# Batch 1's column norms summed on VectorE and GpSimd instead of by TensorE

## The chip, the cores and the metric

One core of one Trainium2 chip. The metric is the device time of one execution in microseconds (us), as the median of several. The profile is one execution; its span is some 2 us shorter than the device time.

## The reference

Two stages: an attention over channels (the softmax of a 256 x 256 matrix per batch, built from normalised q and k) and a feed-forward layer with a maximum over three products.

```python
B, N, C = (4, 6144, 256)
qn = q / (np.linalg.norm(q, axis=1, keepdims=True) + 1e-06)   # norm over the 6144 tokens
kn = k / (np.linalg.norm(k, axis=1, keepdims=True) + 1e-06)
s = kn.transpose(0, 2, 1) @ qn / tau
a = softmax(s)                                                 # ... cut
x = (v @ a).reshape(B * N, C)
h = np.maximum(np.maximum(x @ w1, x @ w2), x @ w3)             # d_ff = 768
out = h @ w_out
```

The kernel folds `a` into the weights (`aw = a @ w`), so that each chunk of 512 tokens needs only `v @ aw`, the maximum, and `@ w_out`. There are 12 chunks per batch. While a batch runs, the next one's q and k are loaded, squared for the norms, and multiplied into the Gram matrix `k^T q`.

## The kernel before

The norms need, per channel, a sum of squares over 128 partitions x 48 token groups. ScalarE squares three groups at a time, GpSimd adds the pieces into an accumulator and folds it to 256 columns, and then something has to add over the 128 partitions. For batch 1 that was TensorE, with a matrix of ones; for batches 2 and 3 ("early", squares run one chunk sooner) it is GpSimd.

```python
def norms(b):                       # batch 1: TensorE adds over the partitions
    n_ps = htile("n_ps")
    accq, acck = accs.pop((b, 0)), accs.pop((b, 1))
    PE.matmul(n_ps[:, :C], lhsT=ones_f, rhs=acck[:, 0:C], ...)
    for j in range(CC):
        PE.matmul(n_ps[:, C + j:C + j + 1], lhsT=accq[:, j * P:(j + 1) * P], rhs=ones_f[:, 0:1], ...)
    # ... cut: Ln and Exp on ScalarE give rkb and rq

def sum_all(b):                     # batches 2 and 3: GpSimd adds over the partitions
    for which in range(2):
        acc = accs[b, which]
        tot = sm.tile([P, C], FP32, name=f"tot{which}")
        POOL.partition_all_reduce(tot, acc[:, 0:C], P, bass_isa.ReduceOp.add)
        accs[b, which] = tot

def norms_all(b):                   # batches 2 and 3: VectorE picks q's diagonal, then Ln, Exp
    for j in range(CC):
        DVE.tensor_tensor_reduce(out=scr, in0=totq[:, j * P:(j + 1) * P], in1=ident, ...,
                                 accum_out=n2q[:, j:j + 1])
    # ... cut: Ln, Exp of totk -> rkb; Ln, Exp of n2q -> rq
```

A chunk is six hidden blocks. Each takes six matmuls into three PSUM buffers; ScalarE copies the first, VectorE takes the maximum with the second and then with the third. Between the blocks, in "gaps", other work is slipped in: the output products of the chunk before, and at the end of a batch the next batch's norms, the scaling of the Gram (`scaled`), the exponential and the row sums. The Gram itself runs as one burst of 48 matmuls ahead of the last chunk. Hidden blocks share six PSUM buffers, the Gram and the output products share two. (PSUM is the memory that TensorE writes its results to; copying a result out of it is called an eviction here. A "weight product" is a part of `a @ w`, a "fold" adds the three 256-column pieces of an accumulator into one, and a "diagonal pick" takes q's sums from a full tile into one column.)

## Time and profile before

| | before |
|---|---|
| device time, median of the executions timed beside the changed kernel | 574.09 us (574.03 to 574.11) |
| span of the profiled execution | 572.1 us (its device time: 573.92 us) |
| TensorE busy | 553.9 us, 97% |
| VectorE, ScalarE, GpSimd busy | 411.1, 309.1, 235.1 us |
| Gram burst of batch 1 starts | 151.75 us |

A timeline line reads: start in us, length in us, engine, line of the program, operation, output <- inputs, shapes, number of instructions merged, and in brackets the idle time before it and what ended it. PE is TensorE, PEld its weight load, DVE VectorE, ACT ScalarE, POOL GpSimd. As TensorE is nearly always busy, only its own order and its waits matter; the prediction shows the lines.

### The profile page before, as it was taken

The numbers are of one execution on the slowest core, as the hardware profiler recorded it, in microseconds if no ns is written. First come the engines' busy times: TensorE is split into PE (matmuls) and PEld (weight loads), VectorE is DVE, ScalarE is ACT, GpSimd is POOL, SyncE is SP. The second block draws the span as 40 slices with busy tenths as digits, with TensorE's granted clock in tenths as the row PEclk, the third lists the DMA queues.
The fourth block names the chain that finished last, engine by engine and source line by source line (L and its number), as shares of the span: only waits on it lengthen the run. The fifth ranks groups of instructions, "written<-read, shape, count | busy, mean of one in ns | idle before, by whom it ended". The sixth has DMA issues, their size and how long they took to land.

```text
span 572.1 us, 9442 instructions
## 1 busy us (share of the span) xinstructions
PE 553.9 (97%) x3349; PEld 330.7 (58%) x3350; DVE 411.1 (72%) x647; ACT 309.1 (54%) x539; POOL 235.1 (41%) x240
## 2 busy tenths in 40 slices
PE   3799999999999999999999999999999999999997
PEld 2665555555755555555575555555575555555566
DVE  0048777877577777777768777777868778778775
ACT  1044567677454576776545467767645444444443
POOL 2443357776730078776560048777750000000000
PEclk9999999999999999999999999999999999999999
DMA  9998998884598168984179339885437323132112
GB/s 143 106 146 129 136 237 126 159 135 116 99 107 160 56 107 158 134 148 110 57 128 151 99 81 140 148 141 98 124 86 154 75 75 109 56 103 64 56 55 76
DMA packets 76960, 65.64 MB, mean 115 GB/s; under 512 B 52464, under 2 KB 62576, under 8 KB 76784
## 3 DMA queue, kind: packets, MB, share of 16 engines
q0 software_dynamic: 19072, 26.48, 38.7%
q1 hardware_dynamic: 57696, 38.41, 23.7%
q8 instruction: 26, 0.43, 0.3%
q14 instruction: 22, 0.18, 0.1%
q10 hardware_dynamic: 144, 0.13, 0.1%
HBM read 78.64 MB, written 25.17 MB: 181 GB/s over the span
## 4 chain that ended last, share of the span: by engine, by line
PE 93%; DMA 5%; POOL 0%; issue 0%; DVE 0%; POOLq 0%
PE h_ps L389 65%; PE o_ps L409 22%; DMA q_sb<-in_q_dram 5%; PE gram L260 3%; PE ew_ps L311 3%; POOL k_sb L99 0%; PE o_ps L434 0%; PE ew_ps L335 0%; PE warm_ps L469 0%; PE vt_ps L372 0%; PE gram L177 0%; PE n_ps L215 0%; DVE ht_sb L395 0%; DVE o_sb L461 0%; PE n_ps L217 0%
## 5 line engine op out<-in xcount | busy, mean ns | idle before, releaser
L389 PE MATMUL h_ps<-vt_sb,aw_sb 128*128 128x512 bf16 (+1 forms) x1764 | 406.7, 375 | 0.1
L389 PEld LDWEIGHTS <-aw_sb 128*128 128x128 bf16 x1764 | 171.8, 98 | 161.3 <-DVE aw_sb L317 2.0
L394 DVE TENSOR_TENSOR s_mx<-h_ps,s_mx 128x512 bf16<-128x512 f32 (+1 forms) x294 | 198.7, 676 | 87.1 <-ACT s_mx L393 86.8
L393 ACT ACTIVATE s_mx<-h_ps 128x512 bf16<-128x512 f32 (+1 forms) x294 | 172.4, 587 | 124.9 <-PE h_ps L389 124.0
L395 DVE TENSOR_TENSOR ht_sb<-h_ps,s_mx 128x512 bf16<-128x512 f32 (+1 forms) x294 | 200.2, 681 | 31.4 <-PE o_ps L409 0.5
L203 POOL TENSOR_TENSOR acc<-acc,sq 128x768 f32<-128x768 f32 x90 | 147.6, 1651 | 70.5 <-ACT sq L197 61.6
L409 PE MATMUL o_ps<-wo_sb,ht_sb 128*128 128x256 bf16 x1128 | 153.9, 273 | 0.0
L409 PEld LDWEIGHTS <-ht_sb 128*128 128x128 bf16 x1128 | 110.4, 98 | 52.0
L412 ACT ACTIVATE o_sb<-o_ps 128x512 f32<-128x512 f32 x94 | 56.1, 597 | 85.3 <-PE o_ps L409 85.3
L110 POOL DMA_DIRECT2D v_sb<-in_v_dram x48 | 27.5, 578 | 37.7 <-DMA vt_sb<-v_sb 35.5
L197 ACT ACTIVATE sq<-q_sb 128x768 bf16<-128x768 fp8e4 x48 | 40.5, 845 | 0.0
L197 ACT ACTIVATE sq<-k_sb 128x768 bf16<-128x768 fp8e4 x48 | 40.1, 835 | 0.0
L200 POOL CAST acc<-sq 128x768 f32<-128x768 bf16 x6 | 4.9, 823 | 68.7 <-ACT sq L197 68.7
L102 POOL DMA_DIRECT2D q_sb<-in_q_dram x33 | 18.4, 564 | 5.1 <-DMA v_sb<-in_v_dram 4.1
L165 PE MATMUL kk<-k_sb 128*128 128x256 fp8e4 x48 | 7.5, 338 | 11.9 <-DVE k_sb L151 6.3
L99 POOL DMA_DIRECT2D k_sb<-in_k_dram x29 | 16.1, 555 | 3.1 <-DMA v_sb<-in_v_dram 1.2
L260 PE MATMUL gram<-k_sb,q_sb 128*128 128x512 fp8e4 x144 | 16.8, 277 | 0.0
L260 PEld LDWEIGHTS <-q_sb 128*128 128x256 fp8e4 x144 | 15.9, 136 | 0.6
L314 ACT ACTIVATE aw_sb<-ew_ps,rinv 128x384 bf16<-128x384 f32 (+1 forms) x24 | 13.2, 555 | 5.5 <-PE ew_ps L311 4.7
L311 PE MATMUL ew_ps<-w_sb,et 128*128 128x384 bf16 (+1 forms) x96 | 15.6, 313 | 0.0
L177 PE MATMUL gram<-k_sb,q_sb 128*128 128x512 fp8e4 x48 | 11.4, 332 | 2.6 <-DMA q_sb<-in_q_dram 2.4
L165 PEld LDWEIGHTS <-k_sb 128*128 128x256 fp8e4 x48 | 6.4, 182 | 12.9 <-DMA k_sb<-in_k_dram 6.6
(67 smaller groups left out, 112.9 us busy)
## 6 DMA issues: line engine op xcount, KB each, us to landing
out_dram<-o_sb SPq DMA_DIRECT2D x41, 512.0 KB, 2.9
v_sb<-in_v_dram POOLq DMA_DIRECT2D x48, 256.0 KB, 4.2
k_sb<-in_k_dram POOLq DMA_DIRECT2D x24, 192.0 KB, 6.0
q_sb<-in_q_dram POOLq DMA_DIRECT2D x24, 192.0 KB, 7.6
out_dram<-o_sb SPq DMA_DIRECT2D x13, 256.0 KB, 2.0
k_sb<-in_k_dram POOLq DMA_DIRECT2D x5, 256.0 KB, 10.8
w_sb<-in_moe_w_dram POOLq DMA_DIRECT2D x9, 128.0 KB, 5.7
kf<-in_k_dram SPq DMA_DIRECT2D x1, 1024.0 KB, 4.8
```

Of the source, the lines that this page charges most:

```text
L102: POOL.dma_start(out=qk[b][0][:, g0:g0 + w, :], in_=q_r[b][:, g0:g0 + w, :])
L110: POOL.dma_start(out=t, in_=v_r[gi // NCH, gi % NCH])
L197: ACT.activation(out=sq, in_=src, func=AF.Square)
L203: POOL.tensor_tensor(out=acc, in0=acc, in1=sq, op=ALU.add)
L260: PE.matmul(g[:, j * C:(j + 1) * C], lhsT=qt[:, tsl, j * P:(j + 1) * P], rhs=kt[:, tsl, :], start=(tp == 0 and j == 0), stop=(tp == NG // ...
L311: PE.matmul(ew[:, :w], lhsT=et[:, j, ic * P:(ic + 1) * P], rhs=w_sb[m][:, j, fsl], start=(j == 0), stop=(j == CC - 1))
L389: PE.matmul(t.rearrange("p (t n) -> p t n", n=P), lhsT=aw[m][:, ic, fsl], rhs=vt[:, tsl, ic, :], start=(ic == 0), stop=(ic == CC - 1))
L393: ACT.activation(out=s_mx, in_=hp[0], func=AF.Copy)
L394: DVE.tensor_tensor(out=s_mx, in0=hp[1], in1=s_mx, op=ALU.max)
L395: DVE.tensor_tensor(out=ht, in0=hp[2], in1=s_mx, op=ALU.max)
L409: PE.matmul(st["ps"][:, half], lhsT=ht[:, fc, t * P:(t + 1) * P], rhs=wo_sb[:, fc, :], start=(fc == 0), stop=(fc == FC - 1))
L412: ACT.activation(out=st["o"][:, t - 1:t + 1, :].rearrange("p t d -> p (t d)"), in_=st["ps"], func=AF.Copy)
```

## The change

The intent is to take the norm matmuls of batch 1 off TensorE. GpSimd alone would be too late for it (an estimate: in the kernel before its folds end at 154.53 + 3.02 = 157.55 us, about 6 us for its library and 3.6 us for two sums would follow, to near 167 us, and ScalarE took up the norms at 159.46), so VectorE adds the last two q squares and does the folds while it is idle in the Gram burst, and a dummy sum makes GpSimd take up its library a chunk ahead.

```diff
+    zero = consts.tile([P, 4], FP32, name="zero")
+    DVE.memset(zero, 0.0)
+    lib = consts.tile([P, 4], FP32, name="lib")
...
-    def norms(b):                       # the TensorE version goes; norms_all is renamed norms
-        n_ps = htile("n_ps")
...
+                    last = not early and s0 == 7 and which == 0
+                    # ... the last q squares of batch 1 are left in a list
             if more and s0 == 7:
-                gaps[5].append(lambda: fold(b + 1))
                 if early:
-                    gaps[5].append(lambda: sum_all(b + 1))
+                    gaps[5].append(lambda: (fold(b + 1, POOL), sum_all(b + 1)))
+                else:
+                    gaps[3].append(lambda: POOL.partition_all_reduce(lib, zero, P, bass_isa.ReduceOp.add))
...
-                    gaps[0].append(lambda: st.update(n=norms(b + 1)))
-                    gaps[1].append(lambda: st.update({"in": scaled(gs, st["n"][0])}))
-                    gaps[2].append(lambda: st.update(e=exp_t(st["in"], st["n"][1])))
+                    gaps[1].append(lambda: st.update(n=norms(b + 1)))
+                    gaps[2].append(lambda: st.update({"in": scaled(gs, st["n"][0])}))
+                    gaps[3].append(lambda: st.update(e=exp_t(st["in"], st["n"][1])))
...
             if more and ch == NCH - 2:
                 if early:
-                    st["n"] = norms_all(b + 1)
+                    st["n"] = norms(b + 1)
+                else:
+                    for which, sq in left:
+                        acc = accs[b + 1, which]
+                        DVE.tensor_tensor(out=acc, in0=acc, in1=sq, op=ALU.add)
+                    fold(b + 1, DVE)
+                    sum_all(b + 1)
                 gs = gram_kq(b + 1)
```

More of the change, by code (lines that the diff above doesn't have):

```diff
@@ L192, with square_piece @@
     accs = {}
-    def square_piece(b, which, g0):
+    def square_piece(b, which, g0, leave=None):
         src = qk[b][which][:, g0:g0 + SQW, :].rearrange("p g c -> p (g c)")
@@ L197, in square_piece @@
         ACT.activation(out=sq, in_=src, func=AF.Square)
-        if g0 == 0:
+        if leave is not None:
+            leave.append((which, sq))
+        elif g0 == 0:
             accs[b, which] = sm.tile([P, SQW * C], FP32, name=f"acc{which}")
@@ L203, in square_piece, with fold @@
             POOL.tensor_tensor(out=acc, in0=acc, in1=sq, op=ALU.add)
-    def fold(b):
+    def fold(b, engine):
         for which in range(2):
@@ L208, in fold @@
             for i in range(1, SQW):
-                POOL.tensor_tensor(out=acc[:, 0:C], in0=acc[:, 0:C], in1=acc[:, i * C:(i + 1) * C], op=ALU.add)
-    def norms(b):
-        n_ps = htile("n_ps")
-        accq, acck = accs.pop((b, 0)), accs.pop((b, 1))
-        PE.matmul(n_ps[:, :C], lhsT=ones_f, rhs=acck[:, 0:C], start=True, stop=False, skip_group_check=True)
-        for j in range(CC):
-            PE.matmul(n_ps[:, C + j:C + j + 1], lhsT=accq[:, j * P:(j + 1) * P], rhs=ones_f[:, 0:1],
-                      start=False, stop=(j == CC - 1), skip_group_check=True)
-        ln = sm.tile([P, C + CC], FP32, name="ln")
-        rkb = sm.tile([P, C], FP32, name="rkb")
-        rq = sm.tile([P, CC], FP32, name="rq")
-        ACT.activation(out=ln, in_=n_ps[:, :C + CC], func=AF.Ln)
-        ACT.activation(out=rkb, in_=ln[:, :C], func=AF.Exp, scale=-0.5)
-        ACT.activation(out=rq, in_=ln[:, C:], func=AF.Exp, scale=-0.5, bias=neg_ln_tau)
-        return rkb, rq
+                engine.tensor_tensor(out=acc[:, 0:C], in0=acc[:, 0:C], in1=acc[:, i * C:(i + 1) * C], op=ALU.add)
     def sum_all(b):
@@ L233, in sum_all, with norms @@
             accs[b, which] = tot
-    def norms_all(b):
+    def norms(b):
         totq, totk = accs.pop((b, 0)), accs.pop((b, 1))
@@ L487 @@
     pending = []
+    left = []
     for b in range(B):
@@ L522 @@
                 for i, (which, g) in enumerate(((1, g0), (1, g0 + SQW), (0, g0), (0, g0 + SQW))):
-                    gaps[(0, 2, 3, 5)[i]].append(lambda which=which, g=g: square_piece(b + 1, which, g))
+                    last = not early and s0 == 7 and which == 0
+                    gaps[(0, 2, 3, 5)[i]].append(
+                        lambda which=which, g=g, last=last: square_piece(b + 1, which, g, left if last else None))
             if more and s0 == 7:
-                gaps[5].append(lambda: fold(b + 1))
                 if early:
-                    gaps[5].append(lambda: sum_all(b + 1))
+                    gaps[5].append(lambda: (fold(b + 1, POOL), sum_all(b + 1)))
+                else:
+                    gaps[3].append(lambda: POOL.partition_all_reduce(lib, zero, P, bass_isa.ReduceOp.add))
             if more and ch == NCH - 1:
```

## The prediction

> **What bounds the kernel now.** I read the page first: engines, then the chain that ended last.
>
> ```profile
> PE 553.9 (97%) x3349; PEld 330.7 (58%) x3350; DVE 411.1 (72%) x647; ACT 309.1 (54%) x539; POOL 235.1 (41%) x240
> PE 93%; DMA 5%; POOL 0%; issue 0%; DVE 0%; POOLq 0%
> ```
>
> TensorE is busy for 97% of the span and is 93% of the chain, at full granted clock in every slice. So the change can only win TensorE time it removes or bubbles it closes, and can only lose by making TensorE wait. It touches one place, the end of batch 0, where batch 1's norms are made; batches 2 and 3 already use the other method (sums over partitions on GpSimd). So the timeline of TensorE there for batch 1, and then for batch 2, which shows what the same stretch costs without the norm matmuls:
>
> ```profile
> 157.19 1.47 PE L389 MATMUL h_ps<-vt_sb,aw_sb 128*128 128x512 bf16 x6
> 158.49 0.59 PE L215 MATMUL n_ps<-acc,ones_f 128*128 128x256 f32 x2
> 158.92 0.50 PE L217 MATMUL n_ps<-ones_f,acc 128*128 128x1 f32 x4
> 159.29 1.45 PE L389 MATMUL h_ps<-vt_sb,aw_sb 128*128 128x512 bf16 x6
> ...
> 168.48 2.11 PE L311 MATMUL ew_ps<-w_sb,et 128*128 128x384 bf16 x12
> ...
> 291.98 2.76 PE L389 MATMUL h_ps<-vt_sb,aw_sb 128*128 128x512 bf16 x12
> ...
> 302.48 2.11 PE L311 MATMUL ew_ps<-w_sb,et 128*128 128x384 bf16 x12
> ```
>
> From the first hidden-block matmul after the Gram to the first weight product: 168.48 - 157.19 = 11.29 us in batch 1, 302.48 - 291.98 = 10.50 us in batch 2. The difference, **0.79 us**, is the gap that the norm matmuls make (159.29 - 158.49 = 0.80). Nothing else in TensorE's order differs.
>
> Then the timeline of GpSimd and of VectorE in the model, batch 2:
>
> ```profile
> 278.93 3.01 POOL L209 TENSOR_TENSOR acc<-acc 128x256 f32<-128x256 f32 x4
> 287.99 3.61 POOL L232 PARTITION_ALL_REDUCE tot<-acc  x2 [6.05 <-issue]
> ...
> 289.84 1.22 DVE L241 CUSTOM_DVE_ANT_0 scr<-tot,ident 128x128 f32<-128x128 f32 x1 [1.59 <-POOL tot L232]
> 290.98 0.08 DVE L241 DVE_READ_ACCUMULATOR2_ANT n2q<- 128x1 f32 x1
> 291.09 0.29 DVE L241 CUSTOM_DVE_ANT_0 scr<-tot,ident 128x128 f32<-128x128 f32 x1
> ```
>
> Before the first sum over partitions GpSimd stands still 6.05 us with nothing to wait for (5.69 us in batch 3): taking up its library. Each sum takes 1.8 us. And on batch 1's side:
>
> ```profile
> 148.42 3.25 POOL L203 TENSOR_TENSOR acc<-acc,sq 128x768 f32<-128x768 f32 x2 [2.17 <-ACT sq L197]
> 152.80 1.64 POOL L203 TENSOR_TENSOR acc<-acc,sq 128x768 f32<-128x768 f32 x1 [1.14 <-ACT sq L197]
> 154.53 3.02 POOL L209 TENSOR_TENSOR acc<-acc 128x256 f32<-128x256 f32 x4
> ```
>
> **What the Trainium skill says.** "GPSIMD Engine Reference", section 2.1 Instruction dispatch: the first call to a freshly loaded kernel pays a load of about 6 us, with no visible instruction. The trace agrees (6.05 and 5.69 us of idle). Same page, section 3.1: a two-input add takes GpSimd 1.96 times as long as VectorE. The trace has no such VectorE add; I use the ratio as an estimate. "SBUF — State Buffer", section SBUF: two separate sides: a VectorE operation with two SBUF inputs and a GpSimd operation that reads SBUF hold a shared port pair against each other. The trace agrees: the first diagonal pick above took 1.22 us beside a sum over partitions, the second 0.29 us; and GpSimd's adds beside VectorE's one-SBUF-input maxima keep 1.634 to 1.684 us over all 90.
>
> **The change, step by step.** *Removed from TensorE*: six fp32 matmuls, 0.79 us. This is on the path and is the whole possible gain.
>
> *Library.* The dummy sum is queued on GpSimd behind the last k square's add, which ends at about 148.42 + 1.64 = 150.06. The load then runs to 150.06 + 6.05 = 156.1. The dummy reads 4 columns, so at most the 1.8 us of a real one; I take 1.0. GpSimd is ready at 157.1.
>
> *VectorE in the Gram burst.* It is idle from 153.45 (end of the last maximum) to 158.46, as the Gram holds TensorE from 151.75 to 157.2. It gets two 768-column adds, estimated 1645/1.96 = 0.84 us, and four folds, estimated 726/1.96 = 0.37 us. With 0.1 us between dependent ones that is about 2 x 0.94 + 4 x 0.47 = 3.8 us: q is ready at 156.3, k at 157.2, a microsecond before VectorE is needed. Free.
>
> *Sums.* q from 157.1 to 158.9, k to 160.7. VectorE's diagonal picks are in its queue behind the maxima of block 1. Without the norm matmuls these are at 159.86 and 160.65 (spacings 0.79 and 0.61 as elsewhere); the picks start at 161.26, after both sums, take 2 x 0.3 us, and give n2q at 161.9. ScalarE has Ln and Exp for k done by 161.5; Ln and Exp for q follow at 161.93 and 162.14, and block 2's copy starts at 162.25 instead of 161.07 (its place in batch 2: 295.87 less the offset of 134.80 between the Grams). So ScalarE is some 1.2 us late, with six PSUM buffers, two blocks, to absorb it: block 4 needs block 2's buffers from 164.33; they come free at 162.8, 163.6 and 164.4 against needs of 164.3, 164.8 and 165.2. Free.
>
> *Scaling.* It moves from behind block 1 to behind block 2 on VectorE: 164.27 to 165.02. From here VectorE runs without a gap: maxima of block 3 at 164.93 and 165.72, block 4 at 166.33 and 167.12, reciprocal 167.73, block 5 at 167.89 and 168.68, so its three weight evictions start at 169.29. Without any lateness they would start at 169.84 - 0.79 = 169.05. This **0.24 us** does reach TensorE, for the next batch's first block waits for exactly these evictions already (timeline of weight loads, before):
>
> ```profile
> 171.03 0.14 PEld L389 LDWEIGHTS <-aw_sb 128*128 128x128 bf16 x2 [0.29 <-DVE aw_sb L317]
> 171.56 0.10 PEld L389 LDWEIGHTS <-aw_sb 128*128 128x128 bf16 x1 [0.38 <-DVE aw_sb L317]
> ```
>
> *Later.* GpSimd must take its usual library back at the second batch's first add. It did so before batch 3's squares (idle 6.99 us) while TensorE kept its rhythm of 10.39 us per chunk, so that is hidden. Its V, K and Q loads start some 3 us later, five chunks ahead of use: hidden.
>
> Sum: -0.79 + 0.24 = -0.55 us, or 573.55 us; with something for the port lock between the dummy and VectorE's adds (below), **573.6 us**.
>
> **The rivals.** (1) *The Gram's PSUM buffer becomes a wait.* Gram and output accumulators share two buffers. Before, the third output product of that chunk takes the Gram's buffer, free once scaling ended at 163.06. If it still does, it is wanted at 163.68 and free at 165.05: TensorE stalls 1.4 us, and the kernel ends at about 574.7 (-0.79 + 1.38). Against it: the buffers seem to be handed out in the order in which they come free, and the scaling, one block later, now comes behind ScalarE's copy of the first output half, so that buffer should be taken. I give the stall one chance in five. (2) *The library comes late.* If the load drags (transposes fill the DMA from 152 to 155; the very first library use, at 4.75 us under full DMA, waited 11.0 us), the sums end later, ScalarE stands in Ln, and every microsecond beyond about 0.4 is passed through block 2 to TensorE: 2 us late is some 574.7, 5 us late 577 to 578. For it: that start; against: both 6 us loads, and that the DMA is quiet until 152. One in six. (3) *Port lock*: the dummy can wait for one VectorE add, up to 0.9 us; the sums then end at 161.5, the picks start in their tail, and a further 0.3 us of lateness goes to the weight evictions: 573.9. (4) *All hidden*, the evictions catching up: 573.3.
>
> **Range and chances.** The best possible is 574.1 - 0.79 = 573.3. The middle cases are 573.5 to 573.9, the two bad ones 574.7 and more. So 573.2 to 574.8 should hold it 8 times in 10. Two per cent is 11.5 us, more than ten times what is at stake either way; only a library load gone badly wrong could reach it. Faster 0.002, same 0.99, slower 0.008.
>
> **What would show it right or wrong.** Right: no n_ps lines; a GpSimd idle of about 6 us that starts near 150 and the two sums ending by about 161; VectorE's adds inside the Gram burst, ended by 157.5; the stretch from first hidden block to first weight product 10.5 us; the weight loads' waits on the evictions grown by about a quarter of a microsecond. Wrong: an output product waiting for VectorE's scaled Gram (rival 1); ScalarE's Ln waiting for the sums for over 1.5 us (rival 2); diagonal picks over 0.5 us (rival 3). A time under 573.2 would mean that something outside this stretch moved too.

## The result, and the profile after

The changed kernel takes 573.67 us (573.67 to 573.75, four executions) against 574.09 us (574.03 to 574.11, four). The ratio, computed as the mean time of one kernel's fast runs over that of the other's of the same rounds (so not quite the ratio of the medians), is 0.9993, with a 95% interval of 0.9976 to 1.0011. The four executions of each kernel do not overlap: 0.42 us lie between the medians.

The page of the changed kernel, its engine line:

```profile
PE 552.9 (97%) x3344; PEld 329.1 (58%) x3344; DVE 415.9 (73%) x658; ACT 309.1 (54%) x540; POOL 233.3 (41%) x237
```

TensorE lost 1.0 us of busy time, VectorE gained 4.8 us. A share of busy time says nothing here; the stretch around the Gram does. TensorE's timeline of the changed kernel there (the hidden blocks' line is now L378, the output products' L398, the weight products' L300):

```profile
157.62 2.76 PE L378 MATMUL h_ps<-vt_sb,aw_sb 128*128 128x512 bf16 x12
...
162.82 1.46 PE L378 MATMUL h_ps<-vt_sb,aw_sb 128*128 128x512 bf16 x6
164.12 0.82 PE L398 MATMUL o_ps<-wo_sb,ht_sb 128*128 128x256 bf16 x6
...
168.12 2.11 PE L300 MATMUL ew_ps<-w_sb,et 128*128 128x384 bf16 x12
170.07 1.65 PE L378 MATMUL h_ps<-vt_sb,aw_sb 128*128 128x512 bf16 x6
171.55 2.11 PE L300 MATMUL ew_ps<-w_sb,et 128*128 128x384 bf16 x12
173.50 1.46 PE L378 MATMUL h_ps<-vt_sb,aw_sb 128*128 128x512 bf16 x6
```

The two hidden blocks at 157.62 now follow each other without the norm matmuls. From there to the first weight product: 168.12 - 157.62 = 10.50 us, before 11.29. From the first weight product to the second: 171.55 - 168.12 = 3.43 us. The lines of the kernel before that answer to the last three (its first weight product, at 168.48, is shown in the prediction):

```profile
170.43 1.52 PE L389 MATMUL h_ps<-vt_sb,aw_sb 128*128 128x512 bf16 x6
171.79 2.11 PE L311 MATMUL ew_ps<-w_sb,et 128*128 128x384 bf16 x12
173.74 1.46 PE L389 MATMUL h_ps<-vt_sb,aw_sb 128*128 128x512 bf16 x6
```

There the second stretch was 171.79 - 168.48 = 3.31 us. So 0.79 us came off and 0.12 us came on; over the whole, 173.74 - 157.19 = 16.55 us became 173.50 - 157.62 = 15.88 us, **0.67 us less**. Behind it the two timelines keep the same distance to the end: the last merged output products start at 566.42 before and 566.18 after, 0.24 us apart, as at 173.74 and 173.50. Nothing more is won or lost in the last 400 us.

But the changed kernel's Gram starts 0.44 us later (157.62 - 157.19 is 0.43), and this lies ahead of everything that the change was meant to do. It has two parts. The first comes at the end of batch 0's own Gram, where TensorE waits for the last loads of q, here in the kernel before and in the changed one:

```profile
33.67 0.32 PE L177 MATMUL gram<-k_sb,q_sb 128*128 128x512 fp8e4 x1 [0.16 <-DMA q_sb<-in_q_dram]
```

```profile
33.87 0.32 PE L180 MATMUL gram<-k_sb,q_sb 128*128 128x512 fp8e4 x1 [0.15 <-DMA q_sb<-in_q_dram]
```

TensorE keeps these 0.2 us up to the first chunk, whose hidden blocks are under way from 44.16 and 44.37. (The first K rows also came 0.21 us later: VectorE's conversion of them started at 5.51 and 5.72. But that did not last, as at 27.34 and 27.33 the two timelines are level; the expectation below that blames the first K load is wrong in this.) The rest comes at the first output product. TensorE's timeline of the kernel before:

```profile
50.63 0.82 PE L409 MATMUL o_ps<-wo_sb,ht_sb 128*128 128x256 bf16 x6
```

and the changed kernel's chain that ended last, in order of time (start, length, what), with the same product at its end:

```profile
45.57 5.45 DMA wo_sb<-in_moe_w_out_dram
...
51.07 0.82 PE o_ps L398 x6
```

In the changed kernel's execution this product waited for the load of `w_out`, which landed at 51.02; in the kernel before, the chain runs through TensorE alone there. But there, too, it was close: issued at 45.36 and 5.2 us on its way, the load landed at about 50.56, under 0.1 us before the product. In the changed kernel it was issued 0.21 us later and took 5.45 us, and those 0.25 us more are what TensorE waited for. 0.21 + 0.23 = 0.44 us. So the two profiled spans differ by 572.1 - 571.9 = 0.2 us: 0.67 won, 0.44 lost.

### The profile page after: what moved, and what is told of

Same layout as the page of the kernel before. It is cut to its first block, busy times and chain, and to the rows that moved or that the text cites. A ratio compares the mean times of both kernels' runs of the same rounds, so it can differ in the third digit from the quotient of the medians.

```text
span 571.9 us, 9438 instructions
## 1 busy us (share of the span) xinstructions
PE 552.9 (97%) x3344; PEld 329.1 (58%) x3344; DVE 415.9 (73%) x658; ACT 309.1 (54%) x540; POOL 233.3 (41%) x237
## 4 chain that ended last, share of the span: by engine, by line
PE 90%; DMA 6%; issue 2%; POOL 1%; DVE 0%; POOLq 0%
PE h_ps L378 64%; PE o_ps L398 22%; DMA v_sb<-in_v_dram 3%; PE gram L249 3%; PE ew_ps L300 2%; DMA q_sb<-in_q_dram 1%; DMA wo_sb<-in_moe_w_out_dram 1%; DMA vt_sb<-v_sb 1%; POOL k_sb L99 0%; PE o_ps L423 0%; POOL w_sb L135 0%; POOL q_sb L102 0%; DVE o_sb L450 0%; POOL ident masks.py:199 0%; PE rs_ps L288 0%
## 5 line engine op out<-in xcount | busy, mean ns | idle before, releaser
L378 PE MATMUL h_ps<-vt_sb,aw_sb 128*128 128x512 bf16 (+1 forms) x1764 | 406.6, 375 | 0.1
L378 PEld LDWEIGHTS <-aw_sb 128*128 128x128 bf16 x1764 | 171.7, 98 | 161.7 <-DVE aw_sb L306 2.4
L208 POOL TENSOR_TENSOR acc<-acc,sq 128x768 f32<-128x768 f32 x88 | 144.3, 1649 | 69.3 <-ACT sq L200 53.1
L398 PE MATMUL o_ps<-wo_sb,ht_sb 128*128 128x256 bf16 x1128 | 153.8, 273 | 0.1
L398 PEld LDWEIGHTS <-ht_sb 128*128 128x128 bf16 x1128 | 110.4, 98 | 52.2 <-issue 0.3
L249 PE MATMUL gram<-k_sb,q_sb 128*128 128x512 fp8e4 x144 | 16.8, 276 | 0.0
L221 POOL PARTITION_ALL_REDUCE tot<-acc x6 | 10.9, 1858 | 11.9 <-DVE s_mx L383 6.0
L300 PE MATMUL ew_ps<-w_sb,et 128*128 128x384 bf16 (+1 forms) x96 | 15.6, 313 | 0.0
```

Of the source, the lines that this page charges most:

```text
L208: POOL.tensor_tensor(out=acc, in0=acc, in1=sq, op=ALU.add)
L249: PE.matmul(g[:, j * C:(j + 1) * C], lhsT=qt[:, tsl, j * P:(j + 1) * P], rhs=kt[:, tsl, :], start=(tp == 0 and j == 0), stop=(tp == NG // ...
L300: PE.matmul(ew[:, :w], lhsT=et[:, j, ic * P:(ic + 1) * P], rhs=w_sb[m][:, j, fsl], start=(j == 0), stop=(j == CC - 1))
L378: PE.matmul(t.rearrange("p (t n) -> p t n", n=P), lhsT=aw[m][:, ic, fsl], rhs=vt[:, tsl, ic, :], start=(ic == 0), stop=(ic == CC - 1))
L398: PE.matmul(st["ps"][:, half], lhsT=ht[:, fc, t * P:(t + 1) * P], rhs=wo_sb[:, fc, :], start=(fc == 0), stop=(fc == FC - 1))
```

## The experiments

None gave a result. After the first pair of runs, the double-row matmul mode, which every Gram of this kernel uses, was held back for all kernels. I then made forms of the kernels without the mode. A correct one would have had twice the Gram matmuls, so I kept the Gram's length instead: one token group of each pair, a wrong result.

```diff
-            tsl = slice(2 * tp, 2 * tp + 2)
+            tsl = 2 * tp
...
-                           perf_mode=DR, skip_group_check=True)
+                           skip_group_check=True)
```

Twenty such kernels were handed in, in eleven submissions from 10:10 to 14:30, experiments 1 to 3 and the kernel before among them; no chip ran any. So what follows are designs with what was expected of them, and after each what the two traces say about the question without it.

**1. The changed kernel again, as it is.** No edit. It asks whether the 0.44 us before the Gram belong to the change.

> The changed kernel unaltered, timed again and profiled again, as a control. In the first pair of profiles TensorE gained 0.67 us between the first hidden block after the Gram and the block after the first weight products (16.55 to 15.88 us), but the timed gain was 0.42 us, and the changed kernel's Gram of batch 1 began 0.44 us later (152.19 against 151.75). Theory H, the head only varies from execution to execution (it waits for DMA): the Gram's start will again differ from 152.19 by some tenths, and the timed gain may move towards 0.67. Theory S, the head is slower by some 0.25 us for good: time 573.67 again, gain 0.4.

and, in the half-Gram form,

> The changed kernel without the double-row matmul mode, which could not be run any more: each Gram matmul takes one token group of the pair, so there are as many Gram matmuls of the same width but half the tokens. Wrong result on purpose; baseline of the other half-Gram kernels. If a plain fp8 matmul of 256 columns goes as fast as a double-row one (109 ns each in the first profile), the stretches are again 10.50 us (first hidden block after the Gram to first weight product) and 3.43 us (to the second), and the time is near 573.7; at half the rate the Gram takes 10.5 us and all is longer by some 16 us. In the first pair of profiles TensorE gained 0.67 us over both stretches, but lost 0.44 us in batch 0: 0.21 us because the first K load landed later, 0.23 us in a wait of the first output product for its weights. Theory H, that loss only varies with the DMA from execution to execution: the first output product starts near 50.6 as often as near 51.1. Theory S, the change slows the head for good: near 51.1 again.

Not run. The traces say this much. Nothing in the changed code works before 150 us except one more VectorE memset, 0.06 us long, at 0.93 us; VectorE then waits over 4 us for the first K rows in either kernel. Both parts of the loss are loads that landed later. (That two more small tiles in SBUF shift the addresses of others, and so the loads, is a rival that nothing here tests.) The changed kernel's profiled execution took 573.68 us, like its other three; the profiled one of the kernel before took 573.92, 0.17 us less than its median. If that 0.17 us lay before the Gram, the usual difference there would be 0.44 - 0.17 = 0.27 us, and 0.67 - 0.27 = 0.40 us is about the 0.42 us timed. This fits a head that is usually slower in the changed kernel, but it is an argument from one execution of each, and no mechanism for it is seen. Against mere chance from execution to execution stands that the four timed executions of each kernel lie within 0.08 us. It stays **open**.

**2. Without the dummy sum.** It asks whether the library load starts by itself as soon as GpSimd's queue reaches it, or only once the sum's operands are there.

```diff
-                    gaps[3].append(lambda: POOL.partition_all_reduce(lib, zero, P, bass_isa.ReduceOp.add))
+                    pass
```

> The dummy sum is left out; nothing else. Theory A, the library load starts when the queue reaches the instruction that switches the library, whatever the sum's own operands wait for: the load still starts near 150.5, is over near 156.5, the first real sum starts about 156.6 and the time is that of the changed kernel (573.6 to 573.8); the dummy was not needed. Theory B, the load starts only when the first sum's operands are there (about 156.5): sums end at about 166.3 in place of 160.6, ScalarE's Ln waits that long, TensorE loses about 4.7 us: 578 us. The prediction took B for granted without saying so (it called the dummy the thing that hides the load).

Not run. There is a hint in the switch back to the usual library, in batch 2's squares. GpSimd's timeline of the changed kernel, and ScalarE's squares that feed it:

```profile
195.01 0.82 POOL L205 CAST acc<-sq 128x768 f32<-128x768 bf16 x1 [28.37 <-ACT sq L200]
203.00 1.63 POOL L208 TENSOR_TENSOR acc<-acc,sq 128x768 f32<-128x768 f32 x1 [7.16 <-ACT o_sb L401]
```

```profile
198.93 0.84 ACT L200 ACTIVATE sq<-k_sb 128x768 bf16<-128x768 fp8e4 x1
```

The switch's own record (a pool configuration) stands at 195.9, right after the first operation. The add's last operand was there at 198.93 + 0.84 = 199.77, and the add started at 203.00. Counted from the switch that is 7.1 us, the length of the other loads give or take 1.5 us; counted from the operand it is only 3.2 us, shorter than any load seen whose operands were there (5.69 to 6.05 us of idle, in five cases). So the load probably ran while the operand was still missing, and then the dummy may not be needed. This is an argument: a load of the usual library could simply be short. The other two such switches, before batch 3's squares in either kernel, do not decide it, as their operand is late by as much: 6.95 and 6.97 us from the switch, 3.1 us from the operand. **Open.**

**3. VectorE's diagonal picks one block earlier.** It asks whether the 0.12 us at the weight products come from q's norm on the way through ScalarE.

```diff
+    # ... cut: picks(b) is split off from norms(b)
-                    gaps[1].append(lambda: st.update(n=norms(b + 1)))
+                    gaps[0].append(lambda: st.update(p=picks(b + 1)))
+                    gaps[1].append(lambda: st.update(n=norms(b + 1, st["p"])))
```

> VectorE's two diagonal picks for batch 1 go behind block 0's maxima instead of behind block 1's; ScalarE's part stays where it is. My theory: the weight evictions are late because block 2's copy on ScalarE waits for q's norm, which waits for the picks. With the picks about 1.3 us earlier, q's norm follows k's at once, block 2's copy starts near 161.9 in place of 162.69 (Gram start as in the first profile), VectorE gets idle time back, the evictions start on time (1.36 us after the first weight product, not 1.49), and the stretch from first weight product to the second goes from 3.43 back to 3.31 us: 0.1 us faster than the changed kernel. Rival: the lateness has another cause (the evictions of ScalarE, the second fold): stretch stays 3.43, same time.

Not run, so it is not known whether this beats the changed kernel. The chain is visible in the trace, below.

**4. Sums made 5 us late.** It asks how much lateness of the sums the PSUM buffers can hide.

```diff
-                    gaps[3].append(lambda: POOL.partition_all_reduce(lib, zero, P, bass_isa.ReduceOp.add))
+                    for _ in range(3):          # and zero, lib of 256 columns
+                        gaps[3].append(lambda: POOL.partition_all_reduce(lib, zero, P, bass_isa.ReduceOp.add))
```

> Dose: three dummies of full size in place of one small one, so the real sums end about 3 x 1.85 - 0.56 = 5.0 us later (165.6 in place of 160.6 in the first profile's times). My rule from the prediction: lateness of the sums beyond some 1.2 us (Ln and Exp of k are over at 161.5, q's norm starts at 162.3) goes on through block 2 and the scaling to the weight evictions one for one: 5.0 - 0.8 = about 4.2 us more than the changed kernel, near 577.9 us. Rival: the buffers and VectorE's idle time absorb more of it, so well under 3 us are lost.

Not run; **open**.

## Why the prediction was right

The predicted 573.6 us met 573.67 us. Its steps, checked in the trace, mostly hold to a few hundredths once the Gram's later start (0.44 us) is added to its clock times. But the total agrees partly by luck: the stretch was won a little better than predicted, and the head cost something that was not predicted.

*Norm matmuls gone*: predicted 0.79 us, measured 11.29 - 10.50 = 0.79 us. Right.

*Library and sums.* GpSimd's timeline of the changed kernel:

```profile
148.85 1.65 POOL L208 TENSOR_TENSOR acc<-acc,sq 128x768 f32<-128x768 f32 x1 [2.18 <-ACT sq L200]
156.47 0.56 POOL L522 PARTITION_ALL_REDUCE lib<-zero  x1 [5.98 <-DVE acc L214]
156.96 3.67 POOL L221 PARTITION_ALL_REDUCE tot<-acc  x2
```

The idle of 5.98 us starts behind the last k square's add, at 150.50, as predicted. The profile puts it down to VectorE's folds, but the dummy reads only a tile of zeros written at the start: it waits for nothing, and the idle time is the load. The dummy took 0.56 us where 1.0 was assumed, and the sums ended at 160.63, half a microsecond sooner than predicted on the shifted clock (161.1). Right.

*VectorE in the Gram burst.* Its timeline in the changed kernel:

```profile
153.80 2.01 DVE L544 TENSOR_TENSOR acc<-acc,sq 128x768 f32<-128x768 f32 x2
155.85 2.56 DVE L214 TENSOR_TENSOR acc<-acc 128x256 f32<-128x256 f32 x4
158.89 0.69 DVE L383 TENSOR_TENSOR s_mx<-h_ps,s_mx 128x512 bf16<-128x512 f32 x1 [0.49 <-ACT s_mx L382]
...
161.69 0.28 DVE L230 CUSTOM_DVE_ANT_0 scr<-tot,ident 128x128 f32<-128x128 f32 x1
...
163.30 0.69 DVE L383 TENSOR_TENSOR s_mx<-h_ps,s_mx 128x512 bf16<-128x512 f32 x1 [0.99 <-ACT s_mx L382]
...
164.70 0.75 DVE L257 TENSOR_TENSOR e_in<-gram,rkb 128x256 f32<-128x256 f32 x2
...
168.15 0.16 DVE L290 RECIPROCAL rinv<-rs_ps 128x2 f32<-128x2 f32 x1
168.23 0.67 DVE L383 TENSOR_TENSOR s_mx<-h_ps,s_mx 128x512 bf16<-128x512 f32 x1
...
169.61 1.66 DVE L306 TENSOR_SCALAR aw_sb<-ew_ps,rinv 128x384 bf16<-128x384 f32 x3
```

The adds took 0.95 us each and not the estimated 0.84, and the folds, by the view of their line, this:

```profile
L214 DVE TENSOR_TENSOR acc<-acc x4: 419/425/1303, 155.8 to 157.1; 128x256 f32<-128x256 f32 x4
```

Three (shortest and middle shown) at about 0.42 us against an estimated 0.37, and the last at 1.30 us. It started at 157.1, beside the first real sum on GpSimd (from 156.96). Both work on SBUF alone, and this fits the port lock of rival 3, in a place where I had not looked for it: I expected it between the dummy and VectorE. Two details go beyond the rival: the third fold, from 156.65, ran beside the dummy and still took 0.42 us; and the last fold ended about 0.4 us before q's sum did (157.10 + 1.30 = 158.40; the sum's record, rough as GpSimd's are, ends at 158.85), so it did not wait for the whole sum. The folds therefore ended at 158.41, not at 157.2 plus 0.44 (so the sign "ended by 157.5" failed), and VectorE had 0.49 us to spare before it was needed at 158.89. The conclusion "free" was right with half the margin that was claimed. GpSimd, too, lost nothing, as it was busy with q's sum until the k folds were done.

*Picks, q's norm, scaling.* Predicted with the shift: picks at 161.26 + 0.44 = 161.70, measured 161.69; scaling at 164.71, measured 164.70. Block 2's copy on ScalarE, predicted 162.69:

```profile
160.66 0.42 ACT L236 ACTIVATE lnk<-tot 128x256 f32<-128x256 f32 x1 [0.51 <-POOL tot L221]
...
162.34 0.20 ACT L238 ACTIVATE lnq<-n2q 128x2 f32<-128x2 f32 x1 [0.82 <-DVE n2q L230]
...
162.69 0.58 ACT L382 ACTIVATE s_mx<-h_ps 128x512 bf16<-128x512 f32 x1
```

ScalarE waited 0.51 us for k's sum and then 0.82 us for the picks: the picks, in VectorE's queue behind block 1, set when block 2's copy starts, and not the sums. VectorE then waits 0.99 us for that copy, until 163.30, and has no idle time from there to the weight evictions at 169.61 (lines above). TensorE did not notice: hidden block 4 and all output products keep their distances.

*Weight evictions.* The one mis-sized term that reached TensorE. Predicted lateness 0.24 us; measured against the first weight product, the evictions started 169.61 - 168.12 = 1.49 us after it, before 169.84 - 168.48 = 1.36 us, so 0.13 us late. The difference is mostly the reciprocal: I gave it its whole 0.16 us, but the maximum behind it started 0.08 us after it (lines above). That the lateness reaches TensorE is as predicted. The weight loads of the changed kernel, to be read against the two lines in the prediction (waits of 0.29 and 0.38 us):

```profile
170.27 0.11 PEld L378 LDWEIGHTS <-aw_sb 128*128 128x128 bf16 x2 [0.27 <-DVE aw_sb L306]
170.80 0.11 PEld L378 LDWEIGHTS <-aw_sb 128*128 128x128 bf16 x2 [0.41 <-DVE aw_sb L306]
171.32 0.10 PEld L378 LDWEIGHTS <-aw_sb 128*128 128x128 bf16 x1 [0.41 <-DVE aw_sb L306]
```

There are three waits on VectorE's evictions now, one more, 1.09 us in all where it was 0.67 (the prediction's sign was a quarter of a microsecond more), and the new batch's first hidden block spreads from 1.52 to 1.65 us: 0.13 of it, or 0.12 by the starts of the weight products.

*Sum.* So the stretch gained 0.79 - 0.12 = 0.67 us where 0.55 was predicted; in the profiled pair the gain is smaller by the 0.44 us lost before the Gram, which the prediction did not have. That the timed gain of 0.42 us is smaller for the same reason is likely but not shown (experiment 1). The prediction's last sentence looked for outside changes only on the fast side.

*Rivals.* (1) The third output product, at 164.12, follows its block by 1.30 us like the others and does not wait for the scaling, which ended at 165.45. As only two buffers are shared and one of them still held the Gram, it must have taken that of the first two products, which ScalarE's copy at 163.16 had freed by 163.75. (2) The library was not late: ScalarE's wait for the sums was 0.51 us, under the 1.5 us that I had named. (3) A wait that fits the lock came, elsewhere, and cost TensorE nothing. The switch back to the usual library cost GpSimd 7.16 us of idle time (lines above), and TensorE kept its distance, as predicted.

## What to carry to other kernels

When TensorE never rests, the value of moving work off it can be read from a twin stretch of the same profile that already does without the work: here 11.29 against 10.50 us, exact to the hundredth. Then follow the queues of the engines that take the work over to the next place where TensorE waits for one of them: a lateness of 1.2 us on ScalarE cost the hidden blocks nothing, as their PSUM buffers took it up, but 0.13 us on VectorE came through at the weight evictions, where TensorE had waited before the change too. And with gains below half a microsecond, compare also the part of the program that the change does not touch: here loads that landed later at the start took away two thirds of what was won (0.44 of 0.67 us).

## What the Trainium skill lacked or had wrong

- "GPSIMD Engine Reference", section 3.1 Elementwise, gives 1.96 as the ratio of a two-input add on GpSimd to VectorE (2048 columns). It has no measured ratio for shorter adds. Here it is 1645/954 = 1.72 for 768 columns (one input in bf16) and 726/424 = 1.71 for 256, so VectorE's adds took 0.95 us where the ratio gave 0.84.
- The same page, section 2.1, is right about the load of about 6 us for the library of the sums (5.69 to 6.05 us of idle). The first library of the program, at 4.75 us beside full DMA, took 11.0 and 11.3 us. The page does not say whether the load waits for the operands of the instruction behind it; an add whose operand came 3.9 us after the switch started 7.1 us after it.
- The same page, section 3.2, has only one time for a reduction over partitions, 247,699 ns for `tensor_reduce` at 128 x 2048. The sum over all partitions used here took 1.81 to 1.89 us at 128 x 256 and 0.56 us at 128 x 4 in fp32; no page has it.
- "SBUF — State Buffer", section SBUF: two separate sides, says that VectorE operations with two SBUF inputs and GpSimd's that read SBUF block each other, and that is borne out: a fold took 1.30 us beside a sum on GpSimd and 0.42 us otherwise. That the one that is later waits for the whole instruction of the other is not: the fold ended 0.44 us before the sum's record, and batch 2's first pick (1.22 us, before the change) 0.55 us before it. GpSimd's records are rough, so this is a hint and no more.
